# Fixed order for the first chunks, E3 and E4 of coming chunks moved behind O2, and padded decay loads in a recurrence with two MoE layers

## The chip, the cores and the metric

The kernel runs on one core of one Trainium2 chip. The metric is the device time of one execution in microseconds; lower is better. The core has five engines with instruction streams of their own: TensorE (PE, with its weight loads as PEld), VectorE (DVE), ScalarE (ACT), GpSimd (POOL) and SyncE (SP), which here issues all DMA transfers. Each engine runs its stream in order.

## The reference

Three layers follow one another: a recurrence with decay over 768 steps (4 batches, 8 heads, 40 x 40 states), a dense layer with ELU, and a second layer with eight experts.

```python
for t in range(S):                                  # recurrence, S = 768
    y[:, :, t] = einsum('bhd,bhde->bhe', rt, state)
    Sa = einsum('bhde,bhe->bhd', state, at)
    state = state * wt[:, :, None, :] - einsum('bhd,bhe->bhde', Sa, bt) + einsum('bhd,bhe->bhde', vt, kt)
...
h = x @ w_in; g = elu(h); x2 = g @ w_out            # 3072 tokens, 320 -> 2048 -> 320
...
P = exp(x2 @ w_gate - max); 8 rounds: normalise rows, then columns
out = sum over e of P[:, e] * (relu(x2 @ w1[e]) @ w2[e])   # 8 experts, 320 -> 1024 -> 320
```

The inputs w_in and w_out arrive as float64 bit patterns; the kernel turns them into float32 by shifts on VectorE.

## The kernel before

The recurrence is cut into 24 chunks of 32 steps (C = 32). Inside a chunk the steps are solved at once, between chunks the state is carried on. Each chunk c passes through named stages:

- ldw, ldk, lu, lv (loads of w and a, of k and b, of v, of r), issued on SyncE.
- prep: F, the running product of the decays from the chunk's end, and xE, the one from its start, are scans on VectorE over clamped copies wr and wq of w; aE and the products of k and b with F (KE) are formed on GpSimd, and copied into block form (aB) by ScalarE. prep has five steps, each one token in the order.
- E3: 32 matmuls into bank 3, masked by VectorE into Am, which goes by DMA to Ad in DRAM; LT reads it back in another layout. E1 and E2 transpose KE and xE (into KB and xT). E4: 32 matmuls into banks 0 and 1.
- T (tsolve): a triangular solve on VectorE, for two chunks at a time in the loop, in small steps of two instructions (Tt, Wk); the result goes by DMA through Td to TT. Chunks 0 to 5 (`halves`) solve two halves and correct with a second pass in H2.
- H1 to H4: the state's part (H1 adds to E4's banks), the solve applied (H2), the new state Y (H3), its transposes (H4, Ss). YW scales the state on GpSimd.
- O1, O2, O3a, O3b: the output. O2 makes 32 matmuls into bank 2, masked by VectorE into Gm; O3a (line 566) and O3b (line 577) accumulate into banks 2 and 3.

The second layer (moe1) works on blocks of 256 tokens, that is on two chunks' outputs, which xprep transposes through bank 3 into X. A block has 16 units (blk, f); a unit is eight matmuls of 256 columns (line 620), an activation, and eight more two units later. Its weights must have been converted (w_in_split, w_out_split: a load, three VectorE operations, a ScalarE copy, two GpSimd subtractions; 32 in all).

Two strings write the order out. `order` is run for every chunk c from 6 on and `order2` for chunks 2 to 5; a token `E3+3` is the next step of stage E3 of chunk c + 3, `m` is half a unit of moe1, `p` is three steps of the solve, `G` lets the solve start, `x` and `xl` are steps of xprep. From c = 4 (`fixed`) on, pin_since ties each engine's instructions (not SyncE's) to this order. `start` lists what goes before: chunks 0 and 1, most of the conversions, early stages of chunks 2 to 5. This start and chunks 2 and 3 are not tied; a scheduler with its own time model and priorities (`po`) places them.

After the recurrence the rest of moe1 runs, then the experts: 8 experts x 6 blocks of 512 tokens x 8 columns of 128, in groups of four (begin, mm1, mm2).

Of the kernel before, what the change touches and what calls it, by code (L numbers as in the profile page):

```python
# [1294 lines left out]
```

## Time and profile before

| | us |
|---|---|
| median of 3 runs | 2272.39 |
| lowest, highest | 2266.86, 2277.91 |
| the profiled execution, its own time | 2277.48 |
| its span in the trace | 2275.6 |
| TensorE busy in the span | 2146.8 (94%) |
| VectorE busy in the span | 947.0 (42%) |

Busy time is the time in which an engine has an instruction running; times inside the span count from its start. The granted clock is TensorE's, as a share of its full speed. An idle time's releaser is inferred from semaphore events: where the engine named had long been done, it was another.

### The profile page before, as it was taken

How to read it: one execution, taken by the hardware profiler on the slowest of the kernel's cores; microseconds unless marked ns; L12 is line 12 of the kernel's file. 1: busy time of each engine (PE TensorE's matmuls, PEld its weight loads, DVE VectorE, ACT ScalarE, POOL GpSimd, SP SyncE). 2: the span in 40 equal slices, each digit the busy share in tenths (PEclk: the TensorE clock that was granted, in tenths of full speed). 3: DMA queues.
4: the chain of work that ended last, by engine and by line, in shares of the span. 5: the costliest groups of instructions: out<-in, count | busy, mean ns of one | idle time of the engine just before them, and what ended most of it. 6: DMA issues, size and time to landing. Idle time of an engine off the chain costs nothing.

```text
span 2275.6 us, 48283 instructions
## 1 busy us (share of the span) xinstructions
PE 2146.8 (94%) x20483; PEld 1931.9 (85%) x20483; DVE 947.0 (42%) x1963; ACT 808.4 (36%) x1789; POOL 469.5 (21%) x553
## 2 busy tenths in 40 slices
PE   2478999999999999999999999999999999999998
PEld 2367889888898989898888888888888888888887
DVE  7774777766666622532222222222222222222222
ACT  2243455544555555323324324223223212112111
POOL 5442344434343244002002002002002002001000
PEclk9998899999999999999999999999999999999999
DMA  6544344334443232101002012002002001000000
GB/s 169 151 116 116 91 112 109 102 100 102 107 105 78 60 90 84 45 1 55 19 20 71 21 32 77 26 26 77 26 26 70 1 1 52 1 1 20 24 24 25
DMA packets 179234, 138.34 MB, mean 61 GB/s; under 512 B 103873, under 2 KB 152386, under 8 KB 179010
## 3 DMA queue, kind: packets, MB, share of 16 engines
q1 hardware_dynamic: 179010, 135.17, 21.5%
q8 instruction: 162, 2.65, 0.5%
q14 instruction: 62, 0.51, 0.1%
HBM read 116.63 MB, written 18.48 MB: 59 GB/s over the span
## 4 chain that ended last, share of the span: by engine, by line
PE 75%; DVE 10%; DMA 7%; SPq 3%; issue 2%; ACT 1%; POOL 1%; DVEq 0%; ACTq 0%; POOLq 0%
PE h L856 28%; PE pa L900 10%; PE pa L901 10%; PE pa L899 10%; PE ph L620 4%; PE h L845 2%; DVE Wk L436 2%; DMA LT<-Ad 2%; PE a L647 2%; DVE Tt L429 1%; DMA WA<-in_wa 1%; PE a L648 1%; PE a L649 1%; SPq L448 1%; DMA Ad<-Am 1%
## 5 line engine op out<-in xcount | busy, mean ns | idle before, releaser
L860 DVE SCALAR_TENSOR_TENSOR hl<-h,hh 128x512 fp32r<-128x512 f32 x384 | 265.2, 691 | 765.9 <-ACT hh L859 765.4
L859 ACT ACTIVATE hh<-h 128x512 fp32r<-128x512 f32 x384 | 229.3, 598 | 899.7 <-PE h L856 899.2
L856 PE MATMUL h<-xs,a 128*128 128x512 f32 x2280 | 546.8, 394 | 0.0
L856 PEld LDWEIGHTS h<-xs,a 128*128 128x128 f32 x2280 | 421.1, 188 | 109.1 <-issue 25.4
L899 PE MATMUL pa<-a,hh 128*128 128x320 f32 x1536 | 474.0, 309 | 1.8 <-ACT acc L906 1.6
L900 PE MATMUL pa<-a,hl 128*128 128x320 f32 x1536 | 475.4, 310 | 0.0
L901 PE MATMUL pa<-a,hh 128*128 128x320 f32 x1536 | 475.2, 309 | 0.0
L899 PEld LDWEIGHTS pa<-a,hh 128*128 128x128 f32 x1536 | 288.8, 188 | 7.1 <-ACT acc L906 1.8
L900 PEld LDWEIGHTS pa<-a,hl 128*128 128x128 f32 x1536 | 288.9, 188 | 5.0 <-issue 0.2
L901 PEld LDWEIGHTS pa<-a,hh 128*128 128x128 f32 x1536 | 289.0, 188 | 0.0
L807 POOL TENSOR_TENSOR a<-rw,a 128x384 fp32r<-128x384 f32 x64 | 65.4, 1022 | 1055.3 <-ACT a L805 1046.4
L633 POOL TENSOR_TENSOR gl<-g,gh 128x256 fp32r<-128x256 f32 x192 | 162.5, 846 | 410.6 <-ACT gh L631 296.0
L620 PE MATMUL ph<-X,Wt 128*128 128x256 f32 x1536 | 237.3, 299 | 0.6 <-DVE g L629 0.5
L620 PEld LDWEIGHTS ph<-X,Wt 128*128 128x128 f32 x1536 | 206.3, 199 | 5.1 <-DVE g L629 1.0
L910 DVE SCALAR_TENSOR_TENSOR acc<-pa,Pg,acc 128x320 f32<-128x320 f32 x168 | 80.9, 545 | 184.5 <-PE pa L901 184.5
L629 DVE SCALAR_TENSOR_TENSOR g<-m,ph 128x256 f32<-128x256 f32 x192 | 80.2, 418 | 181.3 <-ACT m L623 164.5
L622 ACT ACTIVATE m<-ph 128x256 f32<-128x256 f32 x192 | 73.5, 383 | 176.7 <-PE ph L620 168.6
L631 ACT ACTIVATE gh<-g 128x256 fp32r<-128x256 f32 x192 | 80.0, 417 | 124.9 <-DVE g L629 123.8
L436 DVE TENSOR_TENSOR Wk<-Wk,Tt 128x132 f32<-128x132 f32 (+24 forms) x279 | 119.2, 427 | 6.5
L856 PE MATMUL h<-X,a 128*128 128x512 f32 x456 | 109.1, 394 | 0.6 <-DVE X L608 0.6
L856 PEld LDWEIGHTS h<-X,a 128*128 128x128 f32 x456 | 84.0, 188 | 22.6 <-issue 5.0
L429 DVE TENSOR_TENSOR Tt<-Wk,LT 128x132 f32<-128x132 f32 (+24 forms) x279 | 92.2, 330 | 19.6 <-DMA LT<-Ad 11.7
(183 smaller groups left out, 2713.0 us busy)
## 6 DMA issues: line engine op xcount, KB each, us to landing
LT<-Ad SPq DMA_DIRECT2D x24, 512.0 KB
rw<-in_moe_w SPq DMA_DIRECT2D x64, 160.0 KB
WA<-in_wa SPq DMA_DIRECT2D x24, 416.0 KB
KE<-in_kb SPq DMA_DIRECT2D x24, 416.0 KB
rw<-in_moe_w SPq DMA_DIRECT2D x64, 128.0 KB
VU<-in_vt SPq DMA_DIRECT2D x24, 320.0 KB
raw<-in_wp SPq DMA_DIRECT2D x16, 384.0 KB
rchk<-in_wp SPq DMA_DIRECT2D x16, 384.0 KB
```

Source lines behind the costliest of these rows:

```text
L429: V.tensor_tensor(out=tv, in0=Wk[:, :, 0:ni, j:j + 1].to_broadcast(sh), in1=LT2[:, :, j, j + 1:C].unsqueeze(2).to_broadcast(sh), op=ALU.mult,)
L436: dve["T"] = V.tensor_tensor(out=Wk[:, :, 0:ni, j + 1:C], in0=Wk[:, :, 0:ni, j + 1:C], in1=tv, op=ALU.subtract)
L620: T.matmul(ph, lhsT=Wt[0:kp, wi, 128 * f:128 * f + 128], rhs=X[0:kp, xi, :], start=(i == 0), stop=(i == 7))
L629: V.scalar_tensor_tensor(out=g, in0=m, scalar=-1.0, in1=ph, op0=ALU.add, op1=ALU.max)
L633: G.tensor_tensor(out=gl, in0=g, in1=gh.bitcast(F32), op=ALU.subtract)
L856: T.matmul(h, lhsT=a1[:, wi, :], rhs=X[bk][:, xi, :], start=(i == 0 and n == 8), stop=(i == n - 1), skip_group_check=(n == 7))
L859: dve["hh"] = A.activation(out=hh, in_=h, func=AF.Relu)
L860: V.scalar_tensor_tensor(out=hl, in0=h, scalar=0.0, in1=hh.bitcast(F32), op0=ALU.max, op1=ALU.subtract)
L899: T.matmul(o, lhsT=hh[:, ts_], rhs=a2[:, 0, :], start=(f == 0), stop=False)
L900: T.matmul(o, lhsT=hl[:, ts_], rhs=a2[:, 0, :], start=False, stop=False)
L901: T.matmul(o, lhsT=hh[:, ts_], rhs=a2[:, 1, :], start=False, stop=(f == NF2 - 1))
L910: V.scalar_tensor_tensor(out=at, in0=o, scalar=Pg[:, tt, e:e + 1], in1=at, op0=ALU.mult, op1=ALU.add)
```

## The change

The start is a new string of single tokens (START), which covers chunks 0 to 3 whole and early stages of chunks 4 to 8, and every engine but SyncE is tied to it. A conversion is three tokens there: d (its load), b (VectorE's part), o (ScalarE's and GpSimd's part); s_10 is up to ten steps of the solve. m in it is half a unit of moe1. The loop starts at chunk 4 with new order strings. In `order`, O3b and O3a of chunk c come as `O3b+-1` and `O3a+-1` at the top of chunk c + 1 (O3b's matmuls before O3a's, so the accumulation flags move), and E4 of chunk c + 1 and E3 of chunk c + 4 stand behind O2; LT of that E3 comes at the next top. `order2`, for chunks 4 and 5, keeps E3+3 in the middle. `order` has 16 m and 16 p as before, `order2` has 14 of each for 16.

The solve always takes two chunks, also chunks 2 and 3, whose LT lies in a tile of its own (two). Loads of w carry a zero column for each row of 32, so that both scans read the load itself: the clamped copies wr and wq end, F is scanned backward, xE's scan has the zero column in its operand, and xE is copied to xC by ScalarE for E2. In chunks 0 and 1 aE and KE are formed by VectorE instead of GpSimd. The range check reads w past the zero columns. In the experts' last group the second matmuls run over two token tiles first and then over the other two.

```diff
+START = """
+lu_0 prep_0*5 E3_0 ldw_2 E3_0 LT_0 E1_0 E2_0 prep_1*5 E3_1*2 LT_1 ldk_2 E4_0 H1_0 E1_1 E2_1 lu_1 d*2 lv_0 b o u_0_1 d b o prep_2 d prep_2*2 ldw_3 b
+s_10 s_11 b prep_2 s_10 o d prep_2 E3_2 b o E3_2 LT_2 E2_2 ldk_3 H2_0 o E1_2 prep_3*2 d*2 H2_0 prep_3 H2_0 O1_0 H3_0 prep_3*2 E3_3 b H3_0 o O1_0 d
+E3_3 YW_1 ldw_4 b E4_1 LT_3 O2_0 H1_1 E1_3 prep_4 ldk_4 E2_3 u_2_3 b o d O2_0 s_10 O3b_0 d lu_2 o H2_1 O3a_0 O3b_0 s_10 H2_1 s_10 prep_4 H2_1 prep_4
+ldw_5 H3_1*2 b o d O1_1*2 H4_1 lv_1 YW_2 O2_1 E4_2 prep_4*2 E3_4 b O3a_1 d O2_1 o prep_5 H1_2 O3b_1 b E3_4 LT_4 o O3b_1 s_9 E1_4 ldk_5 xl E2_4 d
+prep_5 H2_2 prep_5 x*2 b x*2 H2_2 prep_5 m prep_5 o ldw_6 b o d m H2_2 d E3_5 b m E2_5 E3_5 H3_2*2 E1_5 ldk_6 o d O1_2 prep_6*2 lu_3 m O1_2 H4_2 YW_3
+E4_3 m b o d u_4_5 prep_6 H1_3 lv_2 b O2_2 ldw_7 m o O2_2 d LT_5 H2_3 b o d s_10 m H2_3 O3a_2 b o d m O3b_2*2 H2_3 prep_6*2 b prep_7 ldw_8 d o H3_3 m
+E3_6 H3_3 b o d m E3_6 E2_6 E1_6 ldk_7 m b d o LT_6 s_10 prep_7 O1_3 H4_3 lu_4 b YW_4 m d o O1_3 b o lv_3 O2_3 b o d m O2_3 prep_7 b o d m O3a_3 b
+O3b_3 s_20 d b o m d m prep_7 b m o prep_7 m*2 O3b_3 d m o d m x b o b d m x b d o*2 x*2 b o
+"""
+
+
 PLAN = {
     "ps": {"H1": "01", "H2": "1", "H3": "01", "H4": "01", "E1": "23", "E2": "2", "E3": "3", "O1": "23", "O2": "2", "O3": "23", "O4": "3"},
     "pr": {"O1": "01", "O2": "2", "O3": "01", "O4": "3"},
-    "order": "T lv E4 m p E3+3 xl m E3+3 p H1 m p E2+3 LT+3 m p H2 lu+1 m prep+4 p E1+3 ldk+4 m prep+4 p x m prep+4 p H3 m G x H3 p O1 m O1 p H4 m YW+1 prep+4 p O2 ldw+5 x m O2 p m x p O3a m prep+4 p O3b m O3b p m p m p w",
-    "order2": "T lv E4 m p xl m p H1 m p m p H2 lu+1 m prep+4 p H2 m prep+4 p H2 E3+3 m E3+3 E2+3 LT+3 prep+4 p H3 E1+3 ldk+4 x m G H3 x p O1 m O1 p H4 m YW+1 prep+4 p O2 ldw+5 x m O2 p m x p O3a m prep+4 p O3b m O3b p m p m p w",
-    "start": "prep_0 E3_0 LT_0 prep_1 E3_1 LT_1 E1_0 E2_0 lu_0 E1_1 w_5 E2_1 lu_1 E4_0 H1_0 ld_2 prep_2 E3_2 LT_2 lv_0 E1_2 T_0_1 u_2 w_5 ld_3 E2_2 H2_0 t_2 u_3 H3_0 O1_0 O2_0 O3a_0 O3b_0 E4_1 YW_1 H1_1 H2_1 O1_1 w_22 lu_2 ld_4 prep_3 H4_1 lv_1 O2_1 O3a_1 O3b_1 xl H3_1 YW_2 E3_3 LT_3 t_3 E2_3 E1_3 prep_4 E3_4 LT_4 E2_4 E1_4 ld_5 prep_5 ldw_6",
-    "wn": 8,
-    "po": {"prep": 300, "T": -300, "H1": -300},
+    "order": "m LT+3 T O3b+-1 O3a+-1 O3b+-1 p H1 lu+1 m m p p m xl p m E2+3 p p p p lv G prep+4 H2 m m E1+3 ldk+4 prep+4 H3 m m x prep+4 m x H3 O1 prep+4 prep+4 O1 p p H4 p m O2 E4+1 p E3+4 m ldw+5 m E3+4 O2 x YW+1 p x m p p m p m",
+    "order2": "E4 T O3b+-1 m p O3a+-1 H1 lv m O3b+-1 p xl m p H2 lu+1 m p H2 E3+3 E3+3 m prep+4 p H2 m E1+3 ldk+4 x prep+4 E2+3 LT+3 p H3 m x p prep+4 G prep+4 H3 p O1 prep+4 m m O1 p H4 YW+1 p x p m O2 E4+1 E3+4 E3+4 p O2 x ldw+5 m p m p m m",
+    "start": START,
     "tp": ((3, 3), (3, 3)),
-    "fixed": 4,
+    "queue": False,
     "eng": {"RH": "AA", "VU": "AAAA", "YW": "G", "SS": "AA", "UE": "AV", "XT": "A", "KB": "AA", "AB": "AA"},
-    "lead": 3,
...
-    out["wa"] = lay(np.stack([e["w"], e["a"]], 3))
+    ws = np.concatenate([np.zeros_like(e["w"][..., :1]), e["w"]], -1).reshape(N, 2, D, -1)
+    out["wa"] = lay(np.concatenate([ws, np.zeros_like(ws[..., :1]), e["a"].reshape(N, 2, D, -1)], -1))
...
+    def conv_load(kind, i):
+        z = K()
+        z.kind, z.i, z.n = kind, i, 384 if kind == "i" else DM
+        z.raw = cv.tile([128, z.n * e32], I32 if wide else F32, tag="raw", name="raw")
+        SY.dma_start(out=z.raw, in_=wp_d[i] if kind == "i" else wo_d[i * 128:(i + 1) * 128, :])
+        convs.append(z)
...
+    def conv_bits(z):
+        rv = z.raw.rearrange("p (f e) -> p f e", e=e32)
+        z.x = to_f32(rv, cv.tile([128, z.n], F32, tag="tmp", name="tmp", bufs=2)) if wide else rv[:, :, 0]
...
-        V.tensor_scalar(out=wr[0:HR, :, 1:C + 1], in0=wv[:, :, ::-1], scalar1=WLO, scalar2=WHI, op0=ALU.max, op1=ALU.min)
-        V.tensor_scalar(out=wq[0:HR, :, 1:C], in0=wv[:, :, 0:C - 1], scalar1=WLO, scalar2=WHI, op0=ALU.max, op1=ALU.min)
-        yield
-        F = early(c, "F", [NX, C + 1])
-        V.tensor_tensor_scan(out=flat(F)[0:HR], data0=flat(wr)[0:HR], data1=flat(dr)[0:HR], initial=0.0, op0=ALU.mult, op1=ALU.add)
+        dq, z.aB = work.get(c, work[None])
+        yield
+        F = early(c, "F", [NW + 2])
+        prod, rest = (F[0:HR, i:NW + i].rearrange("p (x t) -> p x t", t=C + 1) for i in (1, 2))
+        V.tensor_tensor_scan(out=F[0:HR, 1:NW + 1][:, ::-1], data0=z.WA[0:HR, 1:NW + 1][:, ::-1], data1=flat(dr)[0:HR], initial=0.0, op0=ALU.mult, op1=ALU.add)
         z.Wf = r2.tile([128, NX], F32, tag="Wf", name="Wf", bufs=4)
-        G.tensor_copy(out=z.Wf[0:HR], in_=F[0:HR, :, C])
-        yield
-        V.reciprocal(out=dq[0:HR, :, 0], in_=F[0:HR, :, C])
-        z.xE = early(c, "xE", [NX, C])
-        V.tensor_tensor_scan(out=flat(z.xE)[0:HR], data0=flat(wq)[0:HR], data1=flat(dq)[0:HR], initial=0.0, op0=ALU.mult, op1=ALU.add)
+        G.tensor_copy(out=z.Wf[0:HR], in_=prod[:, :, 0])
+        yield
+        V.reciprocal(out=dq[0:HR, :, 0], in_=prod[:, :, 0])
+        z.xE = early(c, "xE", [NX, C + 1])
+        V.tensor_tensor_scan(out=flat(z.xE)[0:HR], data0=z.WA[0:HR, 0:NW], data1=flat(dq)[0:HR], initial=0.0, op0=ALU.mult, op1=ALU.add)
         z.aE = r2.tile([128, NG, B * C], F32, tag="aE", name="aE", bufs=4)
-        G.tensor_tensor(out=z.aE[0:HR].rearrange("p g t -> p (g t)"), in0=z.WA[0:HR, 1].rearrange("p g t -> p (g t)"), in1=flat(z.xE)[0:HR], op=ALU.mult)
-        yield
+        (V if c < 2 else G).tensor_tensor(out=z.aE[0:HR].rearrange("p g (b t) -> p (g b) t", t=C), in0=z.WA[0:HR, NW + 1:].rearrange("p (x t) -> p x t", t=C), in1=z.xE[0:HR, :, 0:C], op=ALU.mult)
+        yield
+        z.xC = early(c, "xC", [NG, B * C])
         for j in range(2):
             p = slice(64 * j, 64 * j + D)
             cp("AB", j, z.aB[p].rearrange("p g u j t -> p (g u) j t")[:, :, j, :], z.aE[p].rearrange("p g (u t) -> p (g u) t", u=2))
+        A.copy(out=z.xC[0:HR].rearrange("p g (b t) -> p (g b) t", t=C), in_=z.xE[0:HR, :, 0:C])
         yield
         kv = z.KE[0:HR].rearrange("p g u (b k t) -> p (g u b) k t", b=2, k=2)
-        fr = F[0:HR, :, 0:C][:, :, ::-1]
+        fr = rest[:, :, 0:C]
         for kb in range(2):
-            G.tensor_tensor(out=kv[:, :, kb, :], in0=kv[:, :, kb, :], in1=fr, op=ALU.mult)
+            (V if c < 2 else G).tensor_tensor(out=kv[:, :, kb, :], in0=kv[:, :, kb, :], in1=fr, op=ALU.mult)
...
-        xv = z.xE.rearrange("p (g b) t -> p g (b t)", g=NG)
+        xv = z.xC
...
-        SY.dma_start(out=flat(LTs[:, c % 3]), in_=dap(st[c].Ad, 0, [[C * C, B * H], [0, 4], [1, C * C]]))
+        SY.dma_start(out=flat(two[:, c - 2, 0:C] if c in (2, 3) else LTs[:, c % 3]), in_=dap(st[c].Ad, 0, [[C * C, B * H], [0, 4], [1, C * C]]))
...
-        LT2 = LTs[:, x0:x0 + n] if x0 + n <= 3 else LTs[:, ::-2]
+        LT2 = two[:, :, 0:C] if cs[0] == 2 else LTs[:, x0:x0 + n] if x0 + n <= 3 else LTs[:, ::-2]
         Wk = WkT
         tmp = r1.tile([128, 160], F32, tag="Tt", name="Tt")
-        w0 = 0 if n == 2 else cs[0] % 2
-        Wk = Wk[:, w0:w0 + n]
...
+        s, z.begun = not hasattr(z, "begun"), True
         for j in range(2):
             for g in range(NG):
                 for bb in range(B):
-                    T.matmul(PO[j][C * bb:C * bb + C, D * g:D * g + D], lhsT=z.rO[64 * (bb % 2):64 * (bb % 2) + D, bb // 2, j, g, :], rhs=Ss[64 * (bb % 2):64 * (bb % 2) + D, g, bb // 2, j, :], start=(g == 0), stop=False, skip_group_check=True)
+                    T.matmul(PO[j][C * bb:C * bb + C, D * g:D * g + D], lhsT=z.rO[64 * (bb % 2):64 * (bb % 2) + D, bb // 2, j, g, :], rhs=Ss[64 * (bb % 2):64 * (bb % 2) + D, g, bb // 2, j, :], start=(s and g == 0), stop=not s, skip_group_check=True)
...
-                    T.matmul(PO[j][64 * u:64 * u + 64, D * g:D * g + D], lhsT=Gm[:, u, 2 * g + j, :], rhs=z.KB[:, u, D * h:D * h + D], start=(c == 0 and g == 0), stop=True, skip_group_check=True)
+                    T.matmul(PO[j][64 * u:64 * u + 64, D * g:D * g + D], lhsT=Gm[:, u, 2 * g + j, :], rhs=z.KB[:, u, D * h:D * h + D], start=(s and g == 0), stop=(c == 0 or not s), skip_group_check=True)
...
-            seq += [(begin, u[0])] + [(mm1, x) for x in u] + [(mm2, x) for x in u]
+            seq += [(begin, u[0])] + [(mm1, x) for x in u]
+            if u[-1] != units[-1]:
+                seq += [(mm2, x) for x in u]
+            else:
+                seq += [(mm2, x + (p,)) for p in (range(0, TB // 2), range(TB // 2, TB)) for x in u]
...
-            if not wgen:
-                return True
...
+        first_ins = traced()[-1]
+        rec_init()
+        pin_since(first_ins, late_queue=False)
+        for t in tokens(PLAN["start"]):
+            last = traced()[-1]
+            n, *cs = t.split("_")
+            cs = [int(x) for x in cs]
+            if n in cvn:
+                conv(n)
+            elif n == "m":
+                next(mg)
+            elif n in ("x", "xl"):
+                try_xprep(n == "xl")
+            elif n == "u":
+                pump.append(tsolve(*cs))
+                next(pump[-1])
+            elif n == "s":
+                had = len(pump)
+                for _ in range(cs[0]):
+                    if len(pump) == had:
+                        solve(1)
+            else:
+                advance(n, cs[0])
+            pin_since(last, late_queue=PLAN["queue"])
+        if pump:
+            pumping.append(True)
...
-        for c in range(2, NCH + 1):
+        for c in range(4, NCH + 1):
...
+                if c < 5 and o == 4 and n in ("E3", "LT"):
+                    continue
...
-                if c >= PLAN["fixed"]:
-                    pin_since(last)
+                pin_since(last)
```

## Rows read from the trace of the kernel before

**Rows 1.** The page: busy us (share), instructions of each engine:
```profile
PE 2146.8 (94%) x20483; PEld 1931.9 (85%) x20483; DVE 947.0 (42%) x1963; ACT 808.4 (36%) x1789; POOL 469.5 (21%) x553
```

**Rows 2.** Busy us by stretch: PE, PEld, DVE, ACT, POOL; granted clock:
```profile
0.00:136.00 136.00, 58.80 (x910) 47.77 (x910) 97.99 (x205) 36.15 (x77) 68.92 (x93) 1.00 0.57 158
...
136.00:286.20 150.20, 135.78 (x2361) 124.33 (x2358) 91.88 (x212) 66.47 (x162) 52.53 (x62) 0.85 0.40 101
...
0.00:200.00 200.00, 113.76 (x1797) 97.26 (x1798) 139.40 (x304) 63.30 (x142) 94.38 (x122) 0.95 0.52 142
...
310.00:760.00 450.00, 426.46 (x7451) 399.72 (x7452) 318.04 (x750) 228.97 (x585) 179.24 (x206) 0.97 0.39 100
```

**Rows 3.** TensorE in order of time: start, duration, instruction:
```profile
25.88 1.98 PE L365 MATMUL P<-aB,KE 104*64 104x64 f32 x32 [0.18 <-ACT aB L453]
...
136.04 1.65 PE L620 MATMUL ph<-X,Wt 128*128 128x256 f32 x6
...
286.20 1.13 PE L398 MATMUL P<-VU,Am 128*64 128x40 f32 x32
```

**Rows 4.** TensorE's waits, 0 to 300 us: total us, times, longest:
```profile
PE R L577 <- DVE Gm L367: 6.8, 2, 3.6
...
PE P L494 <- DVE RH L485: 5.3, 2, 3.5
...
PE P L603 <- DVE yt L580: 3.1, 1, 3.1
```

**Rows 5.** TensorE's waits, 300 to 760 us:
```profile
PE P L566 <- ACT m L623: 12.2, 10, 1.3
...
PE P L566 <- DVE X L608: 6.5, 8, 1.1
```

**Rows 6.** VectorE in order of time:
```profile
5.21 0.41 DVE L316 TENSOR_SCALAR wr<-WA 104x512 f32<-104x512 f32 x1
...
517.32 0.25 DVE L436 TENSOR_TENSOR Wk<-Wk,Tt 128x108 f32<-128x108 f32 x1
...
518.30 1.24 DVE L436 TENSOR_TENSOR Wk<-Wk,Tt 128x96 f32<-128x96 f32 x1
...
525.07 1.22 DVE L367 TENSOR_TENSOR Gm<-P,cst 128x1024 f32<-128x1024 f32 x1
```

**Rows 7.** TensorE in order of time, steady part:
```profile
492.98 0.76 PE L566 MATMUL P<-Ss,rO 40*32 40x40 f32 x32 [0.78 <-DVE X L608]
...
495.68 1.94 PE L577 MATMUL P<-KB,Gm 128*64 128x40 f32 x32
...
512.58 0.91 PE L347 MATMUL P<-cst,KE 104*128 104x104 f32 x8
...
521.88 1.15 PE L365 MATMUL P<-rB,uE 80*64 80x64 f32 x32
...
526.39 0.78 PE L566 MATMUL P<-Ss,rO 40*32 40x40 f32 x64 [1.26 <-ACT m L623]
...
528.25 1.13 PE L577 MATMUL P<-KB,Gm 128*64 128x40 f32 x32
...
776.04 0.79 PE L566 MATMUL P<-Ss,rO 40*32 40x40 f32 x64
```

**Rows 8.** GpSimd in order of time:
```profile
42.66 2.30 POOL L337 TENSOR_TENSOR KE<-KE,F 104x512 f32<-104x512 f32 x2 [4.15 <-DMA KE<-in_kb]
...
518.11 1.32 POOL L328 TENSOR_TENSOR aE<-WA,xE 104x512 f32<-104x512 f32 x1
```

**Rows 9.** SyncE's DMA queue in order of time:
```profile
37.34 0.40 SPq L296 DMA_DIRECT2D KE<-in_kb  x1
```

**Rows 10.** Groups by line, 0 to 286.2 us: busy us, mean ns of one:
```profile
L620 PE MATMUL ph<-X,Wt 128*128 128x256 f32 x208 | 38.7, 334 | 0.1
...
L316 DVE TENSOR_SCALAR wr<-WA 104x512 f32<-104x512 f32 x10 | 4.2, 423 | 6.1 <-DMA WA<-in_wa 6.1
...
L317 DVE TENSOR_SCALAR wq<-WA 104x496 f32<-104x496 f32 x10 | 4.6, 464 | 0.0
```

More of the change, by code (lines that the diff above doesn't have):

```diff
@@ L118, in build @@
     V, A, G, T, SY = nc.vector, nc.scalar, nc.gpsimd, nc.tensor, nc.sync
-    PINNED = {x.engine for x in (V, A, G, T)}
+    PINNED = {x.engine for x in (V, A, G, T)} | ({SY.engine} if PLAN["queue"] else set())
     pins = {}
@@ L123, in traced, with pin_since @@
         return nc.cur_bb.bb.instructions
-    def pin_since(last, only=None):
+    def pin_since(last, only=None, late_queue=True):
         ins = traced()
@@ L257, in build @@
     CI = C // 4
-    work = {None: (wr, wq, dq, aB)}
+    NW = 4 * NG * (C + 1)
+    work = {None: (dq, aB)}
+    two = sp.tile([128, 2, C + 1, C], F32, name="two")
     def rec_init():
-        for t in (wr, wq, dr, dq):
+        for t in (dr, dq):
             V.memset(t, 0.0)
-        work[1] = (early(1, "wr", [4 * NG, C + 1]), early(1, "wq", [4 * NG, C]), early(1, "dq", [4 * NG, C]), early(1, "aB", [NG * 2 * 2, 64]).rearrange("p (g u j) t -> p g u j t", u=2, j=2))
+        work[1] = (early(1, "dq", [4 * NG, C + 1]), early(1, "aB", [NG * 2 * 2, 64]).rearrange("p (g u j) t -> p g u j t", u=2, j=2))
         for t in work[1]:
@@ L890, in phase_b, with mm2 @@
         xh = c1.tile([128, NBLK, 512], F32R, name="xh")
-        def mm2(e, bk, f):
-            hh, hl = pend.pop((e, bk, f))
+        def mm2(e, bk, f, part=range(TB)):
+            hh, hl = pend[(e, bk, f)]
             _, a2 = ring[(e, f)]
-            for t in range(TB):
+            for t in part:
                 if f == 0:
@@ L1150, in build @@
         mg = msteps()
-        cvd = set()
-        wi_ = [(w_in_split, i, 128) for i in range(NF1)]
-        wo_ = [(w_out_split, i) for i in range(NF1)]
-        k0 = PLAN["lead"]
-        wgen = wi_[:k0]
-        for i in range(NF1):
-            wgen += wi_[k0 + i:k0 + i + 1] + wo_[i:i + 1]
+        wgen = [(k, i) for i in range(NF1) for k in "io"]
         fns = dict(ld=loads, ldw=loadw, ldk=loadk, lu=loadv, lv=loads2, prep=prep, H1=H1, H2=H2, H3=H3, H4=H4, E1=E1, E2=E2, E3=E3, E4=E4, T=tsolve, O1=O1, O2=O2, O3a=O3a, O3b=O3b, YW=YW, LT=LT)
         done = {("ld", 0), ("ld", 1)}
-        def step(n, c):
-            if 0 <= c < NCH and (n, c) not in done:
-                po = PLAN["po"].get(n, 0)
-                with tc.high_priority(offset=po) if po else ExitStack():
-                    run_all(fns[n](c) or ())
-                done.add((n, c))
         going = {}
@@ L1182, in solve @@
                     pump.pop(0)
-                    pumping.pop()
+                    if pumping:
+                        pumping.pop()
+        cvn = dict(d=0, b=0, o=0)
         def conv(n):
-            for _ in range(n):
-                if wgen:
-                    fn, *ar = wgen.pop(0)
-                    cvd.add(("i" if fn is w_in_split else "o", ar[0]))
-                    with tc.issue_after(dve["A"].ins) if "A" in dve else ExitStack():
-                        fn(*ar)
-                    if not wgen:
-                        cvx.close()
-                        late.append(moe.enter_context(tc.tile_pool(name="late", bufs=1)))
@@ new lines, in conv, with tokens @@
+            if i < len(wgen):
+                conv_load(*wgen[i]) if n == "d" else (conv_bits if n == "b" else conv_out)(convs[i])
+                cvn[n] += 1
+                if n == "o" and i + 1 == len(wgen):
+                    cvx.close()
+                    late.append(moe.enter_context(tc.tile_pool(name="late", bufs=1)))
+        def tokens(x):
+            for t in x.split():
+                t, k = (t + "*1").split("*")[:2]
+                yield from [t] * int(k)
+        first_ins = traced()[-1]
@@ L1221, in build @@
+        if pump:
+            pumping.append(True)
+        for c in range(2):
+            st.pop(c)
+        orders = [[(t.split("+")[0], int((t + "+0").split("+")[1])) for t in tokens(PLAN[n])] for n in ("order", "order2")]
         acc = pk = 0
-        for c in range(2, NCH + 1):
+        for c in range(4, NCH + 1):
             if c == 5:
```

98 lines of the change are left out of this document (35 added, 63 removed).

## The prediction

> **What bounds the kernel now.** I read the page's first line, then the busy times by stretch, then TensorE's waits, then the order of its instructions. TensorE is busy for 2146.8 of 2275.6 us [rows 1], so the kernel is bound by it and only its idle time and its slow time can be won. The stretches say where these lie [rows 2]. Up to 136 us it is busy for 58.8 us and idle for 77.2. From 136 to 286.2 us it is idle for 14.4, and the granted clock is 0.85, which is (1 - 0.85) x 150.2 = 22.5 us of full speed lost. From 310 to 760 us it is idle for 23.5 and loses 0.03 x 450 = 13.5 to the clock. The second half has no such loss, and the change leaves its work alone.
>
> The two ends of the early part are marked by instructions [rows 3]: E3 of chunk 0 starts at 25.88 us, the first dense matmul (the first unit of moe1) at 136.04, chunk 6's E4 at 286.20. Before 136 us the waits that recur are those of O3b for Gm (6.8 us), of H2 for RH (5.3) and of xprep for yt (3.1) [rows 4]: the recurrence of chunks 0 and 1, one thing after another, with VectorE serving it late. In the steady part nearly all idle time has one place: O3a, 12.2 + 6.5 = 18.7 us in 18 waits [rows 5]. Their named releasers are long done. O3a writes banks 2 and 3, and bank 2 holds O2's product until VectorE has masked it into Gm: that mask runs from 525.07 for 1.22 us, to 526.29 [rows 6], and O3a starts at 526.39 after 1.26 us idle [rows 7]. In the chunks of the double wait it also waits for xprep in bank 3 (0.78 us more at 492.98), and O3b then takes 1.94 us against 1.13 at 528.25: TensorE has fallen to its lower level (1.2 instead of 2.4 GHz). At 776.04, where no solve is pumped on VectorE any more, O3a does not wait at all [rows 7].
>
> **The change, part by part.**
>
> *The steady order (chunks 6 on).* It has the same 16 m and 16 p tokens. O3b and O3a of a chunk go to the top of the next, so E4 (1.13 us), E3 (1.15), and six half units of moe1 (an m is about 1.0 us: five of them, with E1, H3, O1 and H4, fill the 9.3 us from 512.58 to 521.88 [rows 7]) stand between O2 and O3. VectorE there has three solve steps, E3's mask and Gm's mask, about 4 us, against some 8 us of TensorE work. So the 18.7 us should go, and with them what the double waits cost in clock, 13.5: 32 us. If the cover fails, that stays as it is (0).
>
> What is late next? E3+4 now comes right behind E4+1, and needs k and b of its chunk. Their load (ldk+4) can only be issued after E1+3 has read the same buffer. On TensorE, E1 ends at 513.49 and O2 at 523.03 [rows 7]; the new order has one m fewer and E4 more in between, so the cover is about 9.6 us. The route: a KE load issued at 37.34 lets GpSimd start at 42.66, 5.3 us later, and its two products take 2.30 [rows 8, 9]; that is 7.7, and aE (1.32 us) [rows 8] and what stands ahead on SyncE, where LT, Wk and Td are, can add up to 4. So E3 is late by between 0 and 2 us in each of the 15 chunks where E3+4 runs: 0 to 30 us. I take 0.5 each, 7, since loads mostly find SyncE free. Steady part: 32 - 7 = 25 us. The moved LT has the time from the next chunk's top to G and more, and is costed at nothing.
>
> *Chunks 0 to 3 in one fixed order.* Three effects. First, the head: the first decays are there by 5.21 us, when VectorE's first clamp starts [rows 6], yet E3_0 starts 20.7 us later. The new order needs behind it F, a reciprocal, xE, aE and two copies, each at most as long as the Gm mask of 1.22 us: 6 us. That is 15 us won. Second, the conversions of w_in and w_out, which the scheduler had put ahead of Gm, RH and yt, stand in chosen places: 6.8 + 5.3 + 3.1 = 15 us [rows 4]; of the other 47 us of idle time I credit 5. So the first dense matmul comes at 136 - 35 = 101 us (bounds: 121 with the head alone, 90 if more goes). Third, the work from there to E4_6. Before, it was 135.8 - 22.5 = 113.3 us at full speed, and 36.9 were lost [rows 2]. After, the text of the order has (22 + 10 + 14) / 2 = 23 units done by chunk 6, where there were 208 / 8 = 26 [rows 10], 6 us less; E4_6 and E3_9 are ahead, 2.3 more; and about 5 us of E stages of chunks 3 and 4 are done before 101. That is 104.6. Of the lost 36.9 I keep three quarters, 28: chunks 2 to 5 are still a chain. E4_6 then starts at 101 + 104.6 + 28 = 234 against 286.2. From 52 us go the three units still owed (6), and 2.3 come back: 48 us. Ends: all 36.9 lost and 121 at the head give 20; nothing lost and 95 give 82.
>
> *Smaller parts.* The clamps wr and wq cost VectorE 423 + 464 ns in each chunk [rows 10]; they end, and so do two memsets. VectorE takes aE and the KE products for chunks 0 and 1 (three operations, each below the 1.32 us that GpSimd needs [rows 8]), and ScalarE one more copy (xC) a chunk, no longer than the Gm mask. The F scan runs backward over its operands; no row shows such a scan, so I bound it by its present form and twice that (VectorE has 132 of 450 us free in the steady part [rows 2], which hides either) and take the present. Loads of w and a are 17 columns longer on 1024. The range check reads w in runs of 32 words: hidden behind the second half, where weights are loaded well ahead. All these at nothing. The solve that always has two chunks has as many steps as the paired one had; for chunks 2 and 3 it halves the number of instructions, which is part of the third effect. Splitting the last group's accumulation only sends two of four stores earlier; at most 1 us, taken as 0.
>
> *Sum.* 48 + 25 = 73 us off 2277.48, the profiled execution's own time: 2204.5. It lies 5.1 above the median of the three runs, of which I take off half: **2202**.
>
> **The rivals.**
>
> *VectorE and GpSimd get in each other's way at the start.* A solve step of two SBUF operands takes 0.25 us at 517.32, and 1.24 at 518.30, ending as GpSimd's aE of 518.11 ends [rows 6, 8]. The first 200 us hold 139.4 us of VectorE work and 94.4 of GpSimd's [rows 2], nearly what the new start string asks for (32 conversions, eight preps, three solves), less 7 for clamps. If the two had to take turns throughout, the string would end at 227 instead of the 150 to 170 that my sum needs, chunks 4 and 5 (about 30 us each) would bring E4_6 to 287, and the start would give nothing: 2275 - 25 = 2250. But the two are busy for 234 us in 200 already, so they do overlap; with half the loss the start gives 25 and the time is 2225, still inside the forecast. The Trainium skill's page "GPSIMD Engine Reference", section Key points, says that GpSimd shares its SBUF interfaces with VectorE and contends with instructions of two SBUF inputs; the pair of rows agrees, and the full turn-taking above is what it would make of the start at worst. Chance of a start gain under 20: 0.12.
>
> *The head does not move.* SyncE is not in the fixed order. If its transfers (Ad, LT, Td, TT) queue behind 32 raw loads, chunk 0's solve starts no earlier whatever the engines' order: the change would not do what it says. Start 10, steady 25: 2240. For it: SyncE's order is the scheduler's as before. Against: the raw loads need freed buffers, so they are spread by the conversions. 0.08.
>
> *KE is late (slower).* The place is E3+4 on TensorE, in order ahead of the next m. Each 1 us beyond the cover costs 15 us, and such a wait costs clock too: 13.5 us over 8 double waits, 1.7 each. With the gains of 48 + 32 = 80, the result is slower by more than 0.5% (above 2284) once the lateness passes 4 us: 15 x (4.3 + 1.7) = 90, 2285. It needs SyncE and GpSimd to add 6 us to the 7.7 of the rows. 0.06. Between 3 and 4 us it is a draw: 0.05.
>
> *Everything lands.* Nothing lost after the first dense matmul, no lateness: 82 + 32, 2164. 0.05.
>
> **Chances and range.** The forecast, 2165 to 2235, has the rest, 0.64. 0.5%, about what a measurement of this kernel tells from no change, is 11 us: faster is below 2261. Faster: 0.64 + 0.12 + 0.08 + 0.05 = 0.89; same 0.05; slower 0.06. The range runs from 2165 to 2250: it leaves out the draw and slower cases, the best case and a little of the first rival, 0.18.
>
> **What would show it.** E3_0 starts near 11 us and the first matmul of moe1 near 101; chunk 6's E4 near 234; O3a has no wait in the steady chunks and the granted clock there is 1.00; E3's matmuls have waits under 1 us for GpSimd's KE. The prediction is wrong if the first dense matmul stays beyond 120, if TensorE's idle time between it and chunk 6 grows well over 30 us, or if E3 waits for KE by microseconds in every chunk.

## The result and the profile after

The changed kernel takes 2249.9 us (median of 4 runs) against 2273.9: ratio 0.9895, 95% interval 0.9866 to 0.9924. It is faster by 24 us, a third of the 73 forecast, and lies just inside the upper end of the range (2250). The profiled execution took 2250.6 us, its span 2248.8.

The page's first line, which answers to [rows 1], and the busy times by stretch (PE, PEld, DVE, ACT, POOL; granted clock), which answer to [rows 2]:

```profile
PE 2137.9 (95%) x20483; PEld 1934.8 (86%) x20483; DVE 928.5 (41%) x1889; ACT 815.0 (36%) x1813; POOL 439.7 (20%) x545
```

```profile
0.00:113.52 113.52, 60.40 (x1146) 52.80 (x1146) 72.80 (x148) 34.84 (x76) 36.26 (x54) 0.81 0.63 163
113.52:258.42 144.90, 125.83 (x2064) 116.33 (x2059) 112.32 (x219) 68.24 (x167) 66.99 (x90) 0.77 0.46 126
150.00:200.00 50.00, 34.84 (x420) 32.27 (x415) 37.36 (x72) 18.21 (x46) 27.90 (x40) 0.74 0.53 148
310.00:760.00 450.00, 425.06 (x7534) 404.44 (x7529) 298.45 (x715) 234.85 (x604) 164.76 (x204) 0.96 0.39 98
```

The steady stretch has gained little: 425.06 us busy at clock 0.96, where before had 426.46 at 0.97; from O3b of chunk 6 to that of chunk 23 it is 510.9 us (289.98 to 800.90), against 517.6 before (312.00 to 829.61). The stretch behind the first dense matmul is slower than forecast: 19.1 us idle, and a clock of 0.77 costs 0.23 x 144.9 = 33 of full speed, 52 together where the forecast kept 28.

TensorE in order of time: E3 of chunk 0, the first dense matmul, then the top of chunk 8 (O3b and O3a of chunk 7, and E1 further on):

```profile
11.44 1.98 PE L383 MATMUL P<-aB,KE 104*64 104x64 f32 x32 [11.44 <-ACT aB L469]
...
113.52 2.08 PE L638 MATMUL ph<-X,Wt 128*128 128x256 f32 x8
...
319.01 1.13 PE L595 MATMUL P<-KB,Gm 128*64 128x40 f32 x32
320.07 0.79 PE L583 MATMUL P<-Ss,rO 40*32 40x40 f32 x64
...
331.58 0.93 PE L365 MATMUL P<-cst,KE 104*128 104x104 f32 x8 [2.40 <-ACT xT L469]
```

The head is as forecast (11.44 against "near 11"), the first dense matmul is not (113.5 against 101). O3a has no wait any more. But E1 has one, which before did not have. TensorE's and ScalarE's waits from 310 to 760 us (total, times, longest):

```profile
PE P L365 <- ACT xT L469: 13.3, 6, 2.9
```

```profile
ACT xT L469 <- DMA yd<-xT: 29.4, 7, 5.3
```

E1 writes banks 2 and 3. Bank 2 holds E2's product until ScalarE has copied it into xT, and ScalarE waits for a store. xT has four buffers: chunk c+3 takes that of chunk c-1, whose output is stored from it by O3b, and O3b of c-1 now stands at the top of chunk c. There the store (yd) comes late on SyncE; ScalarE's copy and SyncE's queue in order of time:

```profile
331.11 0.43 ACT L469 COPY xT<-P 128x320 f32<-128x320 f32 x1 [4.57 <-DMA yd<-xT]
```

```profile
317.05 3.86 SPq L460 DMA_DIRECT2D Td<-Wk  x6
321.10 2.94 SPq L464 DMA_DIRECT2D TT<-Td  x4
324.08 1.17 SPq L460 DMA_DIRECT2D Td<-Wk  x2
325.30 0.61 SPq L408 DMA_DIRECT2D LT<-Ad  x1
326.01 0.54 SPq L603 DMA_DIRECT2D yd<-xT  x1
```

Chunk 7's output is ready at 321.6 (GpSimd's copy of its last columns, 321.32 + 0.24), and its store is issued at 326.0, behind the solve's transfers. This happens in even chunks, where Td and TT are.

Chunk 6's E4 (251.26) is now done in chunk 5, so it no longer marks the same place as in [rows 3]. A fair mark is O3b of chunks 3, 4, 5, before and after:

```profile
216.16 1.13 PE L577 MATMUL P<-KB,Gm 128*64 128x40 f32 x32
...
246.92 1.78 PE L577 MATMUL P<-KB,Gm 128*64 128x40 f32 x32
...
282.08 1.13 PE L577 MATMUL P<-KB,Gm 128*64 128x40 f32 x32
```

```profile
168.08 1.93 PE L595 MATMUL P<-KB,Gm 128*64 128x40 f32 x32
...
226.15 1.13 PE L595 MATMUL P<-KB,Gm 128*64 128x40 f32 x32
...
258.42 1.13 PE L595 MATMUL P<-KB,Gm 128*64 128x40 f32 x32
```

At chunk 3 the lead is 48.1 us, the size of the forecast; at chunk 4 it is 20.8, at chunk 5 23.7. Between chunks 3 and 4 lie 58 us (30.8 before), with the last conversions and the end of the solve of chunks 4 and 5. But the lead at chunk 3 is not all won. The dense matmuls of line 620 (now 638) up to that O3b, before and after:

```profile
0.00:216.16 216.16, 21.81 (x104) 18.38 (x104) 0.94 0.52 142
```

```profile
0.00:168.08 168.08, 12.02 (x56) 10.23 (x56) 0.78 0.61 163
```

Eight are one unit: after is six units behind there, some 12 us at the prediction's 1.0 us for half a unit. At chunk 4 both have 128, at chunk 5 both 192. So about 12 of the 27 us between 48.1 and 20.8 are dense work that before had already done, and the rest is lost time. The conversions themselves have moved. VectorE's second word operation, before up to 136.04 us, and after up to 113.52 and from there to 258.42:

```profile
L205 DVE SCALAR_TENSOR_TENSOR tmp<-raw,tmp 128x384 int32<-128x384 int32 (+1 forms) x30 | 20.1, 674 | 0.4
```

```profile
L215 DVE SCALAR_TENSOR_TENSOR tmp<-raw,tmp 128x384 int32<-128x384 int32 (+1 forms) x12 | 7.6, 631 | 0.4
...
L215 DVE SCALAR_TENSOR_TENSOR tmp<-raw,tmp 128x384 int32<-128x384 int32 (+1 forms) x20 | 15.3, 763 | 0.7
```

Before had 30 of 32 conversions behind it when the dense work began; after has 12, and 20 stand beside chunks 2 to 4.

### The profile page after: what moved, and what is told of

Its sections match the earlier page's. It is cut to its first block, busy times and chain, and to the rows that moved or that the text cites. A ratio compares the mean times of both kernels' runs of the same rounds, so it can differ in the third digit from the quotient of the medians.

```text
span 2248.8 us, 48229 instructions
## 1 busy us (share of the span) xinstructions
PE 2137.9 (95%) x20483; PEld 1934.8 (86%) x20483; DVE 928.5 (41%) x1889; ACT 815.0 (36%) x1813; POOL 439.7 (20%) x545
## 4 chain that ended last, share of the span: by engine, by line
PE 79%; DVE 9%; DMA 4%; issue 2%; ACT 2%; SPq 2%; POOL 1%; DVEq 0%; ACTq 0%; POOLq 0%
PE h L874 28%; PE pa L918 10%; PE pa L919 10%; PE pa L917 10%; PE ph L638 5%; PE h L863 2%; PE a L665 2%; DVE Wk L452 2%; DVE Tt L445 2%; DMA yd<-xT 1%; PE P L534 1%; PE a L666 1%; PE a L667 1%; PE P L383 1%; PE P L510 1%
## 5 line engine op out<-in xcount | busy, mean ns | idle before, releaser
L651 POOL TENSOR_TENSOR gl<-g,gh 128x256 fp32r<-128x256 f32 x192 | 150.1, 782 | 385.1 <-ACT gh L649 305.0
L638 PEld LDWEIGHTS ph<-X,Wt 128*128 128x128 f32 x1536 | 212.2, 205 | 13.1 <-DVE g L647 11.5
L452 DVE TENSOR_TENSOR Wk<-Wk,Tt 128x132 f32<-128x132 f32 (+24 forms) x279 | 109.4, 392 | 8.6
```

The source lines that it names most:

```text
L452: V.tensor_tensor(out=Wk[:, :, 0:ni, j + 1:C], in0=Wk[:, :, 0:ni, j + 1:C], in1=tv, op=ALU.subtract)
L638: T.matmul(ph, lhsT=Wt[0:kp, wi, 128 * f:128 * f + 128], rhs=X[0:kp, xi, :], start=(i == 0), stop=(i == 7))
L651: G.tensor_tensor(out=gl, in0=g, in1=gh.bitcast(F32), op=ALU.subtract)
```

## The experiments

All times are medians; the interval of each ratio to before is about 0.2% (5 us) either way, so differences under 5 us decide nothing. The kernel before, measured beside each group of runs, had medians from 2269 to 2276, so between groups the ratios are the better guide.

**The steady part.** *A fifth xT buffer:*

```diff
-        z.xT = r2.tile([128, 384], F32, tag="xT", name="xT", bufs=4)
+        z.xT = r2.tile([128, 384], F32, tag="xT", name="xT", bufs=5)
```

> The changed kernel with five buffers for xT in place of four. Theory (output store): in every even chunk E1 waits for bank 2, bank 2 for ScalarE's copy into xT, and that copy for the store of the chunk before last's output, which the new order issues only behind SyncE's Td and TT. With a fifth buffer the 13.3 us of waits of E1 for xT are gone, and the granted clock from 310 to 760 us rises from 0.96 to about 0.98, which is 9 us more: 2229 us, at the least 2238. Rival (the wait moves): the next thing late, KE, KB or bank 2 itself, takes the place of xT within the same microseconds: 2247 to 2252.

2226.9 us (ratio 0.9791, 0.9770 to 0.9812). E1 has no wait left between 310 and 760 us, and the stretch does more in the same time (O3b of chunk 6 to that of chunk 23 in 487.3 us, 290.34 to 777.68):

```profile
310.00:760.00 450.00, 435.63 (x7969) 416.04 (x7968) 306.92 (x730) 246.05 (x635) 171.57 (x213) 0.98 0.40 100
```

*The same store off SyncE, with four buffers:*

```diff
-            SY.dma_start(out=yd[c], in_=y)
+            A.dma_start(out=yd[c], in_=y)
```

> The changed kernel with four buffers for xT as it was, but the output store issued by ScalarE in place of SyncE. Theory (the store is late because it stands behind Td and TT on SyncE): E1's 13.3 us of waits for xT go, and the time is 2226 to 2235. Rival (the store's own transfer, about 5 us, is too long for four buffers wherever it is issued): the waits stay above 8 us and the time is 2243 or more.

2227.0 us (0.9785). In the same chunk the store leaves at 324.76 on ScalarE's queue, and the copy into xT no longer waits. So it was the place in SyncE's queue, and a buffer more or another queue cures it alike.

*The old steady order behind the new start:*

```diff
+    "order3": "T lv E4 m p E3+3 xl m E3+3 p H1 m ... O3a m prep+4 p O3b m O3b p m p m p w",
...
+            rest = [("O3b", -1), ("O3a", -1), ("O3b", -1)] if c == PLAN["halves"] else []
+            for n, o in orders[1] if c < PLAN["halves"] else rest + orders[2]:
```

> The changed kernel's start and its chunks 4 and 5, but from chunk 6 on the order of the kernel before (E4 and E3 at the chunk's top, O3a and O3b in their own chunk). Theory (the new steady order is worth nothing as it stands): O3a's 18.7 us of waits come back, E1's 13.3 for xT and the lower clock go, and the time stays at 2245 to 2255. Rival (the steady order gives the 25 us of the prediction and the start gives nothing): 2270 to 2280.

2254.8 us (0.9916, 0.9896 to 0.9935). So the new steady order is worth about 5 us as it stands, no more than the interval, and 2254.8 - 2226.9 = 28 with the store's wait gone. The start, with the smaller parts, is worth 2273.8 - 2254.8 = 19. O3a's 18.7 us of waits did not come back, against what was expected: O3a waits 4.4 us, and the most of it has gone to H4 (TensorE's waits from 310 to 760 us).

```profile
PE P L552 <- DVE Y L543: 14.4, 7, 2.1
PE P L584 <- DVE X L627: 4.4, 7, 1.1
```

**The start: what is between chunk 3 and chunk 4?** *The solve of chunks 4 and 5 earlier:*

```diff
-... ldk_7 m b d o LT_6 s_10 prep_7 O1_3 H4_3 ... O3b_3 s_20 d b
+... ldk_7 m b d o LT_6 s_30 prep_7 O1_3 H4_3 ... O3b_3 d b
```

> The changed kernel with the last 20 steps of the solve of chunks 4 and 5 put together behind chunk 6's LT, 10 of them ahead of O2 of chunk 3, in place of 10 there and 10 behind it. Theory (the late solve): the Td and TT transfers leave at about 160 us in place of 176.28, so the raw loads no longer stand behind them and VectorE's 5.7 us of waits for raw words go; H2 of chunk 4 starts near 188 in place of 198.01, and the time is 2240 to 2245. Rival (VectorE and ScalarE are full of conversions between 160 and 200, whatever comes first): chunk 3's output is 3 to 5 us later, H2 of chunk 4 stays within 3 us of 198, and the time is 2248 to 2255.

2258.7 us (0.9936), a miss for both. H2 of chunk 4 starts at 205.96. Td and TT do leave at 161, but the raw loads stand behind them there just as well. SyncE's queue, then VectorE:

```profile
161.12 4.82 SPq L460 DMA_DIRECT2D Td<-Wk  x6
166.63 2.13 SPq L464 DMA_DIRECT2D TT<-Td  x4
168.81 1.17 SPq L460 DMA_DIRECT2D Td<-Wk  x2
170.08 0.54 SPq L226 DMA_DIRECT2D raw<-in_moe_w_out  x1
```

```profile
173.41 0.33 DVE L214 TENSOR_SCALAR tmp<-raw 128x320 int32<-128x320 int32 x1 [6.16 <-DMA raw<-in_moe_w_out]
```

*Without VectorE's word operations:*

```diff
-        z.x = to_f32(rv, cv.tile([128, z.n], F32, tag="tmp", name="tmp", bufs=2)) if wide else rv[:, :, 0]
+        z.x = rv[:, :, 1].bitcast(F32) if wide else rv[:, :, 0]
```

> The changed kernel without the three VectorE operations of each conversion that make a 32-bit float out of the two words of a weight: the conversions read the high word as it is (this part of the computation is left out, some 55 us of VectorE's work in all, 36 of it after 113 us). Theory (the conversions that came out of the head now stand in the way of chunks 2 to 5): TensorE's waits for VectorE and ScalarE between 150 and 200 us go, H2 of chunk 4 starts before 185 in place of 198.01, and the time is 2225 to 2238. Rival (the start is held by its transfers and by the chain of chunks): H2 of chunk 4 moves by under 5 us and the time stays over 2243.

2249.1 us (0.9888): nothing, and H2 of chunk 4 at 196.61, as the rival had it. VectorE's work from 150 to 200 us falls from 37.36 to 15.42, and TensorE's hardly moves. In place of VectorE's words, ScalarE waits for the raw loads (the row of the stretch, and ScalarE's waits from 113 to 258 us):

```profile
150.00:200.00 50.00, 36.15 (x450) 33.56 (x450) 15.42 (x37) 21.05 (x53) 26.20 (x42) 0.74 0.57 156
```

```profile
ACT WoB L243 <- DMA raw<-in_moe_w_out: 17.9, 7, 4.5
```

*A third raw buffer, loads one conversion ahead:*

```diff
-... lu_1 d*2 lv_0 b o
+... lu_1 d*3 lv_0 b o
-    cv = cvx.enter_context(tc.tile_pool(name="cv", bufs=2, side="right"))
+    cv = cvx.enter_context(tc.tile_pool(name="cv", bufs=3, side="right"))
```

> The changed kernel (four buffers for xT, as it was) with a third buffer for the raw words of a conversion, and each raw load asked for one conversion earlier. Theory (the raw loads pace the start's tail: with two buffers each waits for the conversion before last, and then behind Td and TT on SyncE): the chain of 3.4 + 4.2 us of raw transfers and VectorE's 5.7 us of waits for them between 183 and 197 us go for the most part, H2 of chunk 4 starts near 188 in place of 198.01, and the time is 2240 to 2245. Rival (something else holds chunk 4): H2 of chunk 4 stays within 3 us and the time is 2248 to 2253.

2248.7 us (0.9901): nothing, and H2 of chunk 4 at 198.81, the rival again.

*Neither loads nor word operations* (from the kernel with five xT buffers, two raw buffers):

```diff
-        SY.dma_start(out=z.raw, in_=wp_d[i] if kind == "i" else wo_d[i * 128:(i + 1) * 128, :])
...
+        z.x = flat1[:, 0:z.n]
```

> The kernel with five xT buffers (2226.9 us), its conversions without raw loads and word operations: ScalarE and GpSimd round and subtract one constant tile (this leaves the weights of the first dense layer out). Theory (the conversions as a whole, load, VectorE and the waits between, hold the start): no wait for raw words is left, H2 of chunk 4 starts before 185 in place of 199, the output of chunk 5 (260.4) comes before 248, and the time is 2205 to 2214. Rival (the chain of chunks with its solves, beside which the conversions find room): the output of chunk 5 moves by under 5 us, 2220 to 2229.

2204.5 us (0.9680, 0.9649 to 0.9711), 22 below the kernel with five xT buffers (25 by the ratios). H2 of chunk 4 starts at 179.94; in the kernel with five buffers it stands at 201.30, not at the 199 of the expectation. O3b of chunks 1, 4 and 5, which had been at 102.89, 227.71 and 260.37 there:

```profile
97.08 1.13 PE L594 MATMUL R<-KB,Gm 128*64 128x40 f32 x32
...
203.30 1.13 PE L594 MATMUL P<-KB,Gm 128*64 128x40 f32 x32 [1.24 <-DVE Gm L384]
...
235.56 1.13 PE L594 MATMUL P<-KB,Gm 128*64 128x40 f32 x32
```

The lead is 5.8 us at chunk 1 and 24.4 at chunk 4; most of it grows where the moved conversions are. Two further runs split it. *No word operations, four raw buffers, loads two ahead* (the edits of the run without word operations and of the third raw buffer together, with `bufs=4` and `d*4`), *and word operations without loads* (`z.raw = flat1[:, 0:z.n * e32]`):

> The changed kernel (four xT buffers, 2249.9 us) without the word operations, as once before (the conversions read the high word as it is; that part of the computation is left out), now with four raw buffers and each raw load asked for two conversions earlier. Theory (load and word operations each fill the same time, so that taking one away shows the other): now nothing is left to wait for, and the time falls by most of the 22 us that both together were worth, 2228 to 2236. Rival (the loads' own traffic or their place on SyncE costs the time, however early they are asked for): 2243 to 2250.

> The kernel with five xT buffers (2226.9 us) with all word operations in place but reading one constant tile of raw words, so that no raw load is left (this leaves the weights of the first dense layer out). Theory (either one fills the time): VectorE's conversions remain on the path, and the time stays near 2226.9, at 2219 to 2228. Rival (the loads, late on SyncE and 12.6 MB of traffic beside the chain's Ad, LT, Td and TT, are the whole price): near the 2204.5 of the kernel without either, 2203 to 2210.

2237.4 (0.9846), 12 below the changed kernel (11 by the ratios); and 2216.8 (0.9758), 10 below the kernel with five xT buffers (8 by the ratios). Neither lies in an expected range: the first is just above its theory's, the second between its theory's and its rival's. (The raw loads, 16 of 384 KB and 16 of 320, are 11.5 MB, not 12.6.) So loads and word operations each have a part of the 22 us, of roughly the same size as far as these intervals tell. The words' part showed only in the run that also asked for the loads early; four raw buffers with the word operations in place were not run.

**Moves in the start's order.** *E4, H1 and r of chunk 4 ahead of the last conversions* (`s_20 E4_4 H1_4 lv_4 d b o m`), *20 solve steps behind chunk 1's RH* (`O3b_0 H2_1 s_30 prep_4`), and both, with five xT buffers:

> The kernel with five xT buffers (2226.9 us), and E4, H1 and the r loads of chunk 4 moved ahead of the start's last seven conversions and eight half units, right behind the solve. Theory (chunk 4 stands in fixed order behind conversions that wait for their words): H1's copy into RH no longer follows the last conversion on ScalarE, H2 of chunk 4 starts when TT has landed, near 189 in place of 199, and the time is 2217 to 2222. Rival (the tail's dense work has to be done anyway, before or after): H2 is earlier, but the end is not: 2225 to 2229.

> The kernel with five xT buffers (2226.9 us), and 20 steps of the solve of chunks 2 and 3 moved behind the RH of chunk 1's second pass on VectorE. Theory (the fixed order makes RH wait behind solve steps that wait for the Ad and LT transfers): TensorE's wait of 2.4 to 4.3 us for RH near 82 us is gone, the first dense matmul comes at 110 to 111 in place of 114, and the time is 2222 to 2225. Rival (the solve is then as late as RH was): H2 of chunk 2 waits for TT instead, the first dense matmul moves by under 1 us, 2226 to 2230.

> The two moves of the runs before in one kernel, with five xT buffers. If the gains are those of one chain they add up: H2 of chunk 4 near 186, 2213 to 2219. If chunk 4 is held by the solve and its transfers alone, the head's gain is lost there again and the time is that of the kernel that moves chunk 4 alone.

2228.3, 2226.0 and 2228.9 us (0.9808, 0.9812, 0.9817): no gain. In the first, H2 of chunk 4 starts at 189.75 as expected, but ScalarE's copies into VU now stand behind the same conversions. The second pass comes at 204.11 in place of 208.36, and O3b of chunk 5 at 257.33 in place of 260.37: of 11.6 us 3 are left, and at the end none.

```profile
199.65 0.34 PE L500 MATMUL P<-VU,Am 16*32 16x40 f32 x2 [7.62 <-ACT VU L516]
...
204.11 1.93 PE L510 MATMUL P<-RH,TT 64*64 64x40 f32 x32
```

In the second, the longest wait for RH falls from 2.4 to 0.7 us, but H4 now waits 3.4 us for Y, and the first dense matmul still comes at 115.5 (114.1 without the move).

*The last five conversions spread over chunk 4* (START ends at `O3b_3 d m o`; five `w` tokens in order2), and *no dense unit in START* (its `m` tokens out):

> The kernel with five xT buffers (2226.9 us), the start's order ended behind chunk 3's second output step, its last five conversions spread over chunk 4 behind H1, H2 and E2 there. Theory (the fixed order sets chunk 4 behind conversions): both passes of H2 of chunk 4 come 8 us or more earlier, and the time is 2214 to 2221. Rival (the time is TensorE's work and idle time summed, and a dense unit not done here is done later): chunk 4 is earlier, the time is 2224 to 2230.

> The kernel with five xT buffers (2226.9 us) with all 22 half units of the first dense layer taken out of the start's order; they are done later, so nothing is left out. Theory (the chain alone is what holds chunks 2 to 5): the output of chunk 3 (171.6) moves by under 4 us, TensorE idles where the units were, and they cost 11 x 2 us at the end: 2243 to 2250. Rival (the units and their waits for conversions hold the chain): chunk 3's output is 8 us or more earlier and chunk 4's 15 or more, which pays for the units: 2223 to 2232.

2239.8 (0.9836): slower, though both passes of H2 of chunk 4 come earlier as expected (186.2 and 196.4 in place of 201.3 and 208.4) and O3b of chunk 5 is at 252.6 in place of 260.4. The second block's X is laid where the conversions' tiles were: its transposes come at 230.1 in place of 214.2, the seventeenth dense unit near 241 in place of 229, and by 260 us 160 dense matmuls are done in place of 190. That this is the whole reason is not shown. This order also computes something other than the reference, from a cause that stays open, so its time is a hint at most. And 2287.7 (1.0045): O3b of chunks 2 to 5 comes 6 to 8 us earlier, between the two expectations, so the dense units do hold the chain a little. The total says nothing on this, as the steady order then meets the half units out of step (from 310 to 760 us TensorE waits 15.6 us for g, 1.6 with five xT buffers, and the granted clock is 0.92).

*Third raw buffer, with the output store on ScalarE; and the raw loads there too* (`A.dma_start(out=z.raw, ...)`):

> A version without anything left out: four xT buffers, output store issued by ScalarE (2227.0 us by itself), and a third raw buffer with loads asked for one conversion earlier (worth 1 us by itself in the changed kernel). If the third buffer is worth nothing as long as word operations fill the time: 2224 to 2229. If the steady order's waits had hidden its gain: 2217 to 2222.

> The run before with the raw loads issued by ScalarE as well, so that they no longer stand behind Td and TT on SyncE. Theory (the loads' place on SyncE is a part of the price): H2 of chunk 4 starts near 190 in place of 199 and the time is 2214 to 2221. Rival (VectorE's word operations fill that time, or ScalarE now waits with its own work behind a load whose buffer is not free): 2225 to 2235.

2227.1 (0.9805), so the third buffer is again worth nothing, and 2233.1 us (0.9831): the loads' place on SyncE cannot be bought off that way. H2 of chunk 4 is at 205.4 in the latter.

## Why the prediction was wrong

Of the 73 us forecast 24 came. By the runs above 29 of the missing 49 are the start (48 forecast, 19 measured), 23 the store in the steady order, and 3 go the other way. None of the prediction's own three signs of being wrong came: the first dense matmul is before 120, TensorE's idle time behind it is 19.1 us, and E3 waits for KE nowhere in the steady part. They did not cover the two steps that failed.

**Steady order: the mechanism was right, a wait was missed.** O3a has no wait any more, and the new order is worth 28 us once the store is out of the way, 25 forecast. That the two sums are so close is in part luck, since the terms differ. The granted clock of the stretch, to be 1.00, is 0.98 with the fifth buffer and 1.00 with the store on ScalarE, and yet the two kernels take the same time. In place of "less 7" for KE there are 3.8 us in 3 waits for it with the fifth buffer (none in the changed kernel), and 4.9 at H1 that the profile puts down to issue. So the late-KE rival falls. (Its route is 5.3 + 2.30 = 7.6 us, not 7.7.) The step that failed is the list of what is late next. It named KE alone. O3b was moved past the solve's Td and TT on SyncE together with the store that it issues, and xT was held longer by a chunk's top, and neither was counted. That cost 2249.9 - 2226.9 = 23 us.

**Head: right.** E3 of chunk 0 came 14.4 us earlier (15 forecast), H2 of chunk 0 at 51.3 in place of 67.7.

**"The conversions ... stand in chosen places: 15 us" and "of the lost 36.9 I keep three quarters": wrong.** The first dense matmul won 22.5 us, not 35. Of this 14.4 are E3 of chunk 0; of the 20 that the second effect was to give, 8 came. Beside [rows 4], TensorE's waits for Gm, RH and the transposes of xprep up to 113.52 us:

```profile
PE R L595 <- DVE Gm L385: 0.3, 1, 0.3
...
PE P L510 <- DVE RH L501: 4.9, 2, 4.3
...
PE P L621 <- DVE X L626: 2.2, 1, 2.2
```

Gm's wait went, RH's did not. And from there to O3b of chunk 5 the forecast had 132.6 - 4.1 (that O3b stood 4.1 us before chunk 6's E4) = 128.5 us; it took 144.9. A conversion was costed as a wait that goes when it is moved; it is a load, three word operations, a rounding and two subtractions that have to be somewhere. Before had 30 of them in the head, where TensorE was idle for 77.2 us. After has 20 beside chunks 2 to 4, in fixed order ahead of RH and VU. That their loads and words cost 22 us where they now stand, about 6 of them in the head and the rest behind it, is shown; 19 + 22 = 41 of the 48. That they would have cost less left in the head is argued: no run put them back. Of the other 7 the cause is open: the head has waits of 4.9 us for RH, 2.2 for X and 2.9 that the profile puts down to issue, and the run that took most of RH's wait away gained nothing measurable.

**Rivals.** The time is that of "VectorE and GpSimd take turns" (2250), and the start gave less than its 20 us. But that rival put the whole loss into the start and kept the steady 25, while here 23 of the loss are in the steady order; that the time agrees, and lies inside the range by 0.1 us, is luck. Taking away the word operations, over half of VectorE's work between 150 and 200 us, changed nothing as long as the raw loads stayed. Yet the two engines do hold each other up. After 113.52 us the second word operation took 763 ns in the mean against 631 before it. In the whole start one on 384 columns takes 0.56 us in eleven cases, where no GpSimd instruction is running, and 0.96 to 1.41 us in the five where one is running as it starts. So some of the words' part may be contention; what it cost TensorE no run parted. "The head does not move" named the right resource in the wrong place: SyncE is not in the fixed order and did decide, by the output store and the raw loads, not by the head. An order that fixes SyncE too was not tried.

**Smaller parts: as forecast.** The backward F scan takes what the forward one took. VectorE's KE product for chunk 0 takes 684 ns, where GpSimd needs 2.30 / 2 us [rows 8].

**Best version.** The changed kernel with a fifth xT buffer: 2226.9 us, 2.1% below before; with the store on ScalarE in its place 2227.0.

## What to carry to other kernels

A step that is moved later in an order takes its stores along and keeps every tile that it reads a little longer: count the buffers of each, and look at what its queue holds at the new place. Work taken out of an idle head is not gone: follow where each of its instructions and loads lands, and price them there, load and arithmetic together, since removing one alone can show nothing, as it did for the word operations here. Where several in-order engines share a chain, moving one step ahead of a late one may only hand the wait to the next, as in the moves of the start's order.
